# Split-precision expert products: one kind after the other instead of in turn, one cast by a transfer, one store moved

## The chip, the cores and the metric

One NeuronCore of a Trainium2 chip. The metric is the device time of one execution in microseconds (us), as the median of several runs.

## The reference, cut to what matters

```
x = attention(q, k, v, M_prev, z_prev, beta)     # 2304 tokens x 512
logits = x @ w_gate                              # 8 experts, 288 tokens each, greedily by logit
for e in range(8):
    h = maximum(x[mask_e] @ w1[e], 0)            # 512 -> 1024
    out[mask_e] = h @ w2[e]                      # 1024 -> 512
h = maximum(maximum(out @ m1, out @ m2), out @ m3)   # 512 -> 768, the same weights for all tokens
return h @ w_out                                 # 768 -> 512
```

## The kernel before, in words

The program has two stages. The first (attention, 0 to about 240 us of the span) the change leaves as it is. The second runs the routing and the experts one after the other, p = 0 to 7, each with its T = 288 tokens. A planner (`Plan.run`) orders the whole second stage: each task has a key, an engine, a guessed cost and dependences; at each step it takes the task that can start first, and of equals the one with the lowest key. The table `FK` holds the keys' offsets by kind of task, `R1KEY` that of the second routing round, `YSEQ` is new. What the planner gives is a fixed order of instructions on each engine; the engines then wait for each other only by semaphores.

Every matrix product is made to fp32 accuracy from three products: high by high in fp32r (weights in `whi` or `mh`, data in `xhi`, `hh`, `yh` or `gf`/`gc`), and two in bf16 (high by low and low by high, from `wlo`/`ml` and `xlo`/`hl`/`yl`). `mm3` issues the three in turn (lines 1429, 1431, 1432); the text calls them f, b, b, and a set of three a triple. A triple here streams 288 columns. Per expert there are

- h1: 8 blocks fb of 4 triples (d = 0 to 3), `fh1`, from the tokens into PSUM tile `w`; then ReLU and split into `hh`/`hl` (ACT line 1313, DVE 1319, ACT or DVE 1268),
- y: 8 blocks of 4 triples, `fy`, into four PSUM tiles `acc`; then the split into `yh`/`yl`,
- p: 18 blocks of 4 triples, `fp`, for f = 0 to 5 and three matrices i, into `w`; a maximum over i into `mt` (ACT 1550, DVE 1552) and a split,
- o: 18 triples of 512 columns, `fo`, into `acc`; then a copy and an indirect store by GpSimd's queue (line 1624).

That is 1,088 triples of 288 columns and 108 of 512 over the eight experts. In the order before, f, b and b of a triple stand together, two triples to a task; only the last y block and the first p block have tasks of two f and of four b.

The weights of an expert come in eight transfers of 512 KB (line 1361, queue of SP, tile `wraw`, three buffers). Each is split by halves: ACT casts to `whi` (1370), DVE takes the difference (1376), ACT casts the high part to bf16 (1380). The fourth transfer of expert 0 waits for the tokens' gather (1345). SP also stores each expert's row numbers to memory (`fi`, line 1512, tile `tidx` to `idxd`, 4 bytes at a time) and loads them back in another layout (`fj`, 1516). The weights shared by all tokens, `MH[k]` and `ML[k]` for k = 4 to 11, are split in the same stretch: ACT 1283, DVE 1289, ACT 1294.

Of the kernel before, what the change touches and what calls it, by code (L numbers as in the profile page):

```python
# [17 lines left out]
try:  # L18
# [27 lines left out]
RKEY = (-1000, -23.5)  # L46
FL0 = 3
NFILL = 88
R1, R1KEY = 9, 21.8
NK = 4  # L50
RSLACK = 300
CRIT, PATIENCE = -900, 0
GLAT, WLAT = 8500, 6000
FBUFS = {"wraw": 3, "whi": 4, "wlo": 4, "xo": 1, "xhi": 1, "xlo": 1, "w": 3, "acc": 4, "hh": 3, "hl": 3, "yh": 1, "yl": 1,
         "mt": 2, "ob": 3, "gc": 7, "gf": 2, "gcu": 7, "gfu": 2}
FK = {"m2": -600, "ml": 28.3, "load": -63.7, "w2": 17.1, "wsplit": -3.5, "gather": -148.1, "xt": -126.2, "h1": 0, "y": -46.8, "o": 13.0, "store": 103.5, "idx": -41.5}
# [1191 lines left out]
def experts(g, tc, plan, top, wr, xd, idxd, out):  # L1248
# [32 lines left out]
    for k in range(NK, 12):  # L1281
        def fh(e, k=k):
            A.copy(MH[k], g.W32[k])

        def flow(e, k=k, h=0):
            if h == 0:
                g.slot(k)
            q = slice(512 * h, 512 * h + 512)
            V.tensor_sub(ML[k][:, 0, q], g.W32[k][:, q], MH[k][:, q].bitcast(F32))

        t = add(FK["m2"] + k, {"ACT": act(1024)}, fh)
        for h in range(2):
            low = add(FK["ml"] + .1 * k + .05 * h, {"DVE": dve(512)}, lambda e, f=flow, h=h: f(e, h=h), [t, low, g.rounds[0].tt])
        low = add(FK["ml"] + .1 * k + .07, {"ACT": act(1024)}, lambda e, k=k: A.copy(ML[k][:, 1], MH[k].bitcast(F32)), [low])
        TM[k // 3].append(low)
    bfl, fo_ = Buf(R["acc"]), K()

# [33 lines left out]
    for p in range(E):  # L1331
# [92 lines left out]
            x.tx += list(split(kx + .1 * d, T, lambda o=o: o.pt[:, :T], hi, lambda i, x=x, d=d: x.xl[:, i, d], [td] + x.tx[:1],  # L1424
                               new=x.bx if d == 0 else [], use=[ob[d]] + ([] if d == 0 else x.bx)))

        def mm3(o, w, r, start, stop, part=(0, 1)):
            if 0 in part:
                nc.tensor.matmul(o, w[0], r[0], start=start, stop=False)  # L1429
            if 1 in part:  # L1430
                nc.tensor.matmul(o, w[2], r[1], start=False, stop=False)  # L1431
                nc.tensor.matmul(o, w[1], r[2], start=False, stop=stop)  # L1432

        def tri(h, l, d):
            return h[:, d], l[:, 0, d], l[:, 1, d]
# [6 lines left out]
        x.ty = []  # L1442
        hs = {}
        x.acc = [None] * 4
        ylast, yt = [], []
        for fb in range(8):
            bp, bhh, bhl = Buf(R["w"]), Buf(R["hh"]), Buf(R["hl"])
            o = K()
            kh = k0 + 2 * fb
            t = None  # L1450
            for hf in range(2):
                def fh1(e, x=x, fb=fb, hf=hf, o=o):
                    if hf == 0:
                        o.pt = ps.tile([128, 512], F32, name="w", bufs=FBUFS["w"])
                    for d in (2 * hf, 2 * hf + 1):
                        s = slice(d * 128, d * 128 + 128)
                        mm3(o.pt[:, :T], wts(x.W[fb], s), tri(x.xh, x.xl, d), d == 0, d == 3)

                t = add(kh + FK["h1"] + .1 * hf, {"PE": 760}, fh1, x.tw[fb, 0] + (x.tx[:6] if hf == 0 else x.tx + [t]), new=[bp] if hf == 0 else [],
                        use=([] if hf == 0 else [bp]) + x.bx + list(x.bw[fb]))  # L1460
# [19 lines left out]
            for hf, (fb, ts, o, bhh, bhl) in itertools.product(range(2), yt):  # L1480
                def fy(e, x=x, fb=fb, hf=hf, o=o, part=(0, 1)):
                    for d in (2 * hf, 2 * hf + 1):
                        if fb == 0:
                            x.acc[d] = ps.tile([128, 512], F32, name="acc", bufs=4)
                        s = slice(512 + d * 128, 512 + d * 128 + 128)
                        mm3(x.acc[d][:, :T], wts(x.W[fb], s), (o.a, (o.b[:, 0] if 1 in part else None), (o.b[:, 1] if 1 in part else None)), fb == 0, fb == 7, part)

                ky = k0 + 2 * fb + FK["y"] + .1 * hf if fb < 6 else k0 + 14 + FK["y"] + hf + .1 * (fb - 6)
                for part in ((0,), (1,)) if fb == 7 else ((0, 1),):
                    ylast.append(add(ky + .05 * part[0], {"PE": 270 * (0 in part) + 490 * (1 in part)}, lambda e, f=fy, part=part: f(e, part=part),  # L1490
                                     list(ts if 1 in part else ts[:1]) + x.tw[fb, 1] + ylast[-1:] + ([o[-1] for o in prev.ol] if prev else []),
                                     new=ya[2 * hf:2 * hf + 2] if fb == 0 else [],
                                     use=[bhh, bhl] + list(x.bw[fb]) + (ya[2 * hf:2 * hf + 2] if fb else [])))
# [12 lines left out]
        chunks = range(p * T // 128, (p + 1) * T // 128)
        oa = [Buf(R["acc"]) for _ in chunks]
# [7 lines left out]
            a, z = chunks[0], chunks[-1] + 1  # L1515
            nc.sync.dma_start(idx[:, a:z], idxd[a * 128:z * 128].rearrange("(c q) -> q c", q=128))

        t = add(k0 + FK["idx"], {"SP": 500}, fi, [r.tt] + x.tl[FL0:FL0 + 1], lat=2300)
        x.tidx = add(k0 + FK["idx"] + .1, {"SP": 500}, fj, [t], lat=2300)
        x.tm = []  # L1520
        for f in range(6):
            kf = k0 + 20 + 4 * f
# [2 lines left out]
            for i in range(3):  # L1525
                bp = Buf(R["w"])
                o = K()
                t = None
                for hf in range(2):
                    def fp(e, x=x, f=f, i=i, hf=hf, o=o, part=(0, 1)):  # L1530
                        if hf == 0 and 0 in part:
                            o.pt = ps.tile([128, 512], F32, name="w", bufs=FBUFS["w"])
                        for d in (2 * hf, 2 * hf + 1):
                            s = slice(d * F2 + f * 128, d * F2 + f * 128 + 128)
                            mm3(o.pt[:, :T], msub(i, s.start, 128), tri(x.yh, x.yl, d), d == 0, d == 3, part)

                    for part in ((0,), (1,)) if f == 0 and i == 0 else ((0, 1),):
                        need = x.ty[:6] if hf == 0 else x.ty + [t]
                        if part == (0,):
                            need = x.ty[6 * hf:6 * hf + 6:3] + ([t] if hf else [])  # L1540
                        elif part == (1,):
                            need = need + [t]
                        t = tp = add(kf + i + .1 * hf + .05 * part[0], {"PE": 270 * (0 in part) + 490 * (1 in part)},
                                     lambda e, f=fp, part=part: f(e, part=part), need + TM[i], new=[bp] if hf == 0 and 0 in part else [],
                                     use=([] if hf == 0 and 0 in part else [bp]) + x.by)
# [168 lines left out]
```

## Time and profile before

| | |
|---|---|
| median of 3 runs | 817.12 us (816.01 to 817.22) |
| profiled execution: time / span | 816.3 us / 814.6 us |
| PE busy | 783.8 us, 96% of the span |
| DVE, ACT busy | 578.6 us, 480.7 us |
| routing and start of expert 0 | 244 to 303 us of the span |
| experts, PE without a pause | 303 to 808 us |

The rows below are of the profiled execution, in us from the start of its span unless marked ns. A row of a timeline gives start, duration, engine, line, operation, output<-inputs, and in brackets the idle time of the engine just before it with what ended it. Matmuls overlap: a product's end (start plus duration) against the end of the one before it is what it adds.

### The profile page before, as it was taken

The page shows a single profiled execution, that of the slowest core. Times are in us where ns is not written, and L with a number is a line of the kernel's source. Part 1 is how long each engine was busy: PE and PEld are TensorE (multiplying, and loading weights), DVE is VectorE, ACT ScalarE, POOL GpSimd, SP SyncE. Part 2 cuts the span into 40 slices and gives each one's busy share as a digit, 9 for nine tenths or more (in the row PEclk, how much of TensorE's full clock was granted, in tenths as well). Part 3 has the DMA queues.
Part 4 walks back from the last instruction along what each step waited for, and adds up shares of the span by engine and source line. Part 5 has one row for each costly group of instructions (what it writes and reads, how often), then busy time and mean ns, then how long its engine had stood idle before and what let it go on. Part 6 is the DMA issues. An engine that isn't in the chain of part 4 may idle for free.

```text
span 814.6 us, 18746 instructions
## 1 busy us (share of the span) xinstructions
PE 783.8 (96%) x7022; PEld 623.4 (77%) x7022; DVE 578.6 (71%) x1780; ACT 480.7 (59%) x1238; POOL 107.6 (13%) x239
## 2 busy tenths in 40 slices
PE   8999999999986799999999999999999999999996
PEld 6899899899985567677777777767767777776773
DVE  7799999999557888688668757747856865643421
ACT  4678777777647673674564655546556465835521
POOL 2212222223101100201010210110101012001001
PEclk9999999999995899999999999999999999999999
DMA  7364746565013422322312320411331253421000
GB/s 239 91 220 153 238 130 233 177 219 169 23 60 93 110 51 79 107 79 96 116 53 79 107 79 30 157 54 39 104 107 54 78 134 107 132 25 52 2 1 39
DMA packets 39248, 83.79 MB, mean 103 GB/s; under 512 B 11454, under 2 KB 14198, under 8 KB 39158
## 3 DMA queue, kind: packets, MB, share of 16 engines
q1 hardware_dynamic: 35574, 72.87, 28.8%
q0 software_dynamic: 3584, 9.73, 4.0%
q8 instruction: 55, 0.90, 0.5%
q14 instruction: 35, 0.29, 0.1%
HBM read 72.77 MB, written 9.74 MB: 101 GB/s over the span
## 4 chain that ended last, share of the span: by engine, by line
PE 73%; issue 9%; DVE 8%; DMA 5%; ACT 3%; POOL 1%; SPq 1%; DVEq 0%; POOLq 0%; ACTq 0%
PE w L1431 12%; PE w L1429 12%; PE w L1432 11%; PE av L684 9%; PE acc L1429 6%; PE acc L1431 6%; PE acc L1432 5%; PE st L643 5%; PE rps L590 2%; PE rps L1148 2%; PE rps L543 1%; DMA wraw<-in_wr 1%; DVE junk L456 1%; DMA m2raw<-in_m2w 1%; PE w L1405 1%
## 5 line engine op out<-in xcount | busy, mean ns | idle before, releaser
L1429 PE MATMUL w<-yh,mh 128*128 128x288 f32 x576 | 219.8, 390 | 0.2 <-DVE mt L1552 0.2
L1431 PE MATMUL w<-yl,ml 128*128 128x288 bf16 x576 | 169.4, 296 | 0.0
L1432 PE MATMUL w<-yl,ml 128*128 128x288 bf16 x576 | 163.7, 286 | 0.0
L1429 PEld LDWEIGHTS w<-yh,mh 128*128 128x128 f32 x576 | 107.6, 190 | 17.9 <-DVE mt L1552 0.6
L684 PE MATMUL av<-V,pt 128*128 128x112 f32 (+1 forms) x960 | 105.0, 261 | 1.7 <-DVE nm L456 0.7
L684 PEld LDWEIGHTS av<-V,pt 128*128 128x128 f32 (+1 forms) x960 | 96.9, 173 | 6.4 <-issue 1.6
L1429 PE MATMUL w<-xhi,whi 128*128 128x288 f32 x256 | 100.3, 392 | 0.5 <-DVE xlo L1321 0.5
L1429 PE MATMUL acc<-hh,whi 128*128 128x288 f32 x256 | 95.9, 385 | 0.1
L1376 DVE TENSOR_TENSOR wlo<-wraw,whi 128x512 bf16<-128x512 f32 x128 | 84.2, 686 | 15.2 <-ACT whi L1370 14.4
L1552 DVE TENSOR_TENSOR mt<-w,mt 128x288 f32<-128x288 f32 x96 | 43.7, 455 | 66.3 <-PE w L1432 62.2
L1431 PEld LDWEIGHTS <-ml 128*128 128x128 bf16 x576 | 55.0, 96 | 39.0 <-issue 7.2
L1370 ACT CAST whi<-wraw 128x512 fp32r<-128x512 f32 x128 | 74.5, 617 | 17.4 <-PE acc L1429 9.1
L1431 PE MATMUL w<-xlo,wlo 128*128 128x288 bf16 x256 | 76.8, 300 | 1.9 <-ACT wlo L1380 1.9
L1380 ACT CAST wlo<-whi 128x512 bf16<-128x512 f32 x128 | 76.2, 616 | 0.0
L1431 PEld LDWEIGHTS <-wlo 128*128 128x128 bf16 x512 | 49.4, 96 | 34.4 <-ACT wlo L1380 2.4
L1431 PE MATMUL acc<-hl,wlo 128*128 128x288 bf16 x256 | 75.7, 298 | 0.0
L1432 PE MATMUL w<-xlo,wlo 128*128 128x288 bf16 x256 | 74.0, 289 | 0.0
L456 DVE CUSTOM_DVE_ANT_0 junk<-st,mask 128x512 bf16<-128x512 f32 (+3 forms) x128 | 62.6, 489 | 15.6 <-ACT pt L668 3.8
L1432 PE MATMUL acc<-hl,wlo 128*128 128x288 bf16 x256 | 73.1, 288 | 0.1
L1345 POOL DMA_INDIRECT xg<-xd,tidx x24 | 30.1, 1253 | 255.7 <-PE w L1432 233.3
L670 ACT ACTIVATE pt<-st 128x512 f32<-128x512 f32 x96 | 53.3, 601 | 14.2 <-PE st L643 13.2
L1432 PEld LDWEIGHTS <-ml 128*128 128x128 bf16 x576 | 57.1, 99 | 0.6
(283 smaller groups left out, 1699.2 us busy)
## 6 DMA issues: line engine op xcount, KB each, us to landing
wraw<-in_wr SPq DMA_DIRECT2D x64, 512.0 KB, 4.3
m2raw<-in_m2w SPq DMA_DIRECT2D x12, 512.0 KB, 5.2
V<-in_v SPq DMA_DIRECT2D x16, 365.0 KB, 5.3
KR<-in_kN SPq DMA_DIRECT2D x16, 288.0 KB, 3.1
QN<-in_qN SPq DMA_DIRECT2D x16, 288.0 KB, 3.1
vt<-in_vT SPq DMA_DIRECT2D x16, 288.0 KB, 5.1
xd<-x SPq DMA_DIRECT2D x16, 256.0 KB, 2.5
m2raw<-in_m2w SPq DMA_DIRECT2D x12, 256.0 KB, 3.1
```

Of the source, the lines that this page charges most:

```text
L456: V.tensor_tensor_reduce(out=junk[:, :w], in0=o.s[x][:, c:c + w], in1=m, scale=1.0, scalar=-3.0e38, op0=OP.add, op1=OP.max, accum_out=r.nm ...
L643: PE.matmul(d[:kr, c:c + z - a], neg[q, :kr] if wt is None else wt[q, k], mv[q, a:z], start=x == 0, stop=x == 3)
L670: A.activation(r.PT[:, i, 512 * gi:512 * gi + 512], o.t[i], AF.Exp, scale=0.125)
L684: PE.matmul(AV[:m, i, j * C:j * C + w], r.PT[:, i, o:o + m], r.V[:, c:c + w], start=kb == 0, stop=kb == j)
L1345: g.gather = G.indirect_dma_start(out=x.xg[:96, c], out_offset=None, in_=xd, in_offset=bass.IndirectOffsetOnAxis(ap=r.tidx[:96, c:c + 1], ...
L1370: A.copy(x.W[fb][0][:, q], x.RAW[fb][:, q])
L1376: V.tensor_sub(x.W[fb][1][:, 0, q], x.RAW[fb][:, q], x.W[fb][0][:, q].bitcast(F32))
L1380: A.copy(x.W[fb][1][:, 1, q], x.W[fb][0][:, q].bitcast(F32))
L1429: nc.tensor.matmul(o, w[0], r[0], start=start, stop=False)
L1431: nc.tensor.matmul(o, w[2], r[1], start=False, stop=False)
L1432: nc.tensor.matmul(o, w[1], r[2], start=False, stop=stop)
L1552: V.tensor_max(q.mt, o.pt[:, :T], q.mt)
```

## The change

Line numbers of the changed kernel are higher by up to 18 (1429 becomes 1441, 1431 and 1432 become 1443 and 1444, 1361 becomes 1371, 1512 and 1516 become 1535 and 1539).

```diff
-R1, R1KEY = 9, 21.8
+R1, R1KEY = 9, 19.9
+YSEQ = ((0, 0, (0, 1, 2, 3)), (0, 1, (0, 1)), (1, 0, (0, 1)), (1, 1, (0, 1)), (0, 1, (2, 3)), (1, 0, (2, 3)), (1, 1, (2, 3)))
-FK = {"m2": -600, "ml": 28.3, "load": -63.7, "w2": 17.1, ...
+FK = {"m2": -600, "ml": 28.9, "load": -59.3, "w2": -38.7, ...
...
+        if k == NK:
+            def fhb(e, k=k):
+                g.slot(k)
+                G.dma_start(ML[k][:, 1], MH[k].bitcast(F32))
+
+            hb = add(-699, {"POOL": 1100}, fhb, [t], lat=8000)
...
+        if k > NK:
+            low = add(FK["ml"] + .1 * k + .07, {"ACT": act(1024)}, lambda e, k=k: A.copy(ML[k][:, 1], MH[k].bitcast(F32)), [low])
+        else:
+            TM[k // 3].append(hb)
...
-        def mm3(o, w, r, start, stop, part=(0, 1)):
-            if 0 in part:
+        ALL, HALF = ((0, (0, 1, 2, 3)), (1, (0, 1, 2, 3))), ((0, (0, 1)), (1, (0, 1)), (0, (2, 3)), (1, (2, 3)))
+
+        def mms(part, o, w, r, start, stop):
+            if part == 0:
                 nc.tensor.matmul(o, w[0], r[0], start=start, stop=False)
-            if 1 in part:
+            else:
                 nc.tensor.matmul(o, w[2], r[1], start=False, stop=False)
                 nc.tensor.matmul(o, w[1], r[2], start=False, stop=stop)
...
-            for hf in range(2):
+            for n, (part, ds) in enumerate(HALF if fb == 0 and p == 0 else ALL):
...
-                    for d in (2 * hf, 2 * hf + 1):
+                    for d in ds:
                         s = slice(d * 128, d * 128 + 128)
-                        mm3(o.pt[:, :T], wts(x.W[fb], s), tri(x.xh, x.xl, d), d == 0, d == 3)
+                        mms(part, o.pt[:, :T], wts(x.W[fb], s), tri(x.xh, x.xl, d), d == 0, d == 3)
...
+            seq = [(i, part, ds) for i in range(len(yt)) for part, ds in (HALF if fb == 0 else ALL)]
+            if fb == 7:
+                seq = YSEQ
...
-        t = add(k0 + FK["idx"], {"SP": 500}, fi, [r.tt] + x.tl[FL0:FL0 + 1], lat=2300)
-        x.tidx = add(k0 + FK["idx"] + .1, {"SP": 500}, fj, [t], lat=2300)
+        t = add(k0 + FK["idx"], {"SP": 500}, fi, [r.tt] + (x.tl[FL0:FL0 + 1] if p else x.tl[7:]), lat=11000)
+        x.tidx = add(k0 + FK["idx"] + .1, {"SP": 500}, fj, [t], lat=5000)
...
-                for hf in range(2):
+                for n, (part, ds) in enumerate(HALF if f == 0 else ALL):
...
-                    mm3(x.oc[ci], [a[:, w:w + 128] for a in (h.t, h.u[:, 0], h.u[:, 1])], msub(3, s.start, DM), f == 0, f == 5)
+                    for part in range(2):
+                        mms(part, x.oc[ci], [a[:, w:w + 128] for a in (h.t, h.u[:, 0], h.u[:, 1])], msub(3, s.start, DM), f == 0, f == 5)
```

A block of h1, y or p is now one task of its four f (`part` 0) and one of its eight b (`part` 1); `HALF` blocks are cut in two by d. The triples of o keep their order. `ML[4]`'s high part is cast by a transfer from SBUF to SBUF on GpSimd's queue, no longer by ACT. The numbers in `FK` shift other tasks; `w2` lets the second half of a weight block be split directly behind the first.

The order on PE, at a p block of the second expert (tile `w`; `mh6` to `mh8` and `mh0` to `mh2` are pieces of the shared weights). Before:

```order
L1429 MATMUL w_5136<-yh_4903,mh6_4130 128x288
L1431 LDWEIGHTS ml_4594
L1431 MATMUL w_5136<-yl_4904,ml_4594 128x288
L1432 LDWEIGHTS ml_4594
L1432 MATMUL w_5136<-yl_4904,ml_4594 128x288
L1429 MATMUL w_5136<-yh_4903,mh7_4131 128x288
```

and after the change, the same kind of place:

```order
L1441 MATMUL w_5235<-yh_4901,mh6_4130 128x288
L1441 MATMUL w_5235<-yh_4901,mh7_4131 128x288 x2
L1441 MATMUL w_5235<-yh_4901,mh8_4132 128x288
L1441 MATMUL w_5243<-yh_4901,mh0_973 128x288
L1441 MATMUL w_5243<-yh_4901,mh1_1162 128x288
L1441 MATMUL w_5243<-yh_4901,mh2_1437 128x288 x2
L1443 LDWEIGHTS ml_4620
L1443 MATMUL w_5235<-yl_4902,ml_4620 128x288
L1444 LDWEIGHTS ml_4620
L1444 MATMUL w_5235<-yl_4902,ml_4620 128x288
```

The planner has put the f tasks of two blocks together: eight f into two tiles `w`, and behind them sixteen b. Over the second stage, an f of 288 columns stood directly behind another 46 times before and 887 times now; directly behind a routing product of 8 columns or fewer, or a transpose, 74 times and 46 times, a b 10 and 34 times.

The order on SP, from the sixth weight transfer of expert 0 (ISA rows set the address; `ei` is the number of the second expert). Before:

```order
L1361 DMA wraw<-in_wr 128x1024
L1512 DMA idxd<-tidx 96x3x1
L1361 ISA
L1361 DMA wraw<-in_wr 128x1024
L1516 DMA idx<-idxd 128x2x1
L1361 ISA
L1361 DMA wraw<-in_wr 128x1024
L1337 TENSOR_LOAD ei
```

and now:

```order
L1371 DMA wraw<-in_wr 128x1024
L1371 ISA
L1371 DMA wraw<-in_wr 128x1024
L1371 ISA
L1371 DMA wraw<-in_wr 128x1024
L1535 DMA idxd<-tidx 96x3x1
L1539 DMA idx<-idxd 128x2x1
L1347 TENSOR_LOAD ei
```

The store and the load of the row numbers have moved behind the seventh and the eighth weight transfer. On POOL the casting transfer stands between the attention's last stores and the first gather:

```order
L873 DMA xd<-xl 128x4x128
L873 DMA xd<-xl 64x128
L1296 DMA ml<-mh_4128 128x1024
L1355 DMA xg<-xd,tidx 96x512 x6
L1641 MEMSET spacer 1x1
```

Nothing else on POOL has moved.

## Rows read from the trace of the kernel before

**Rows 1.** Busy time by stretch: us, then busy (xcount) by engine, PEclk, DMA, GB/s
```profile
244.00:272.00 28.00, 16.35 (x208) 14.24 (x208) 20.65 (x86) 15.32 (x37) 7.25 (x5) 0.65 0.35 88
272.00:303.00 31.00, 28.52 (x231) 21.43 (x231) 26.38 (x49) 25.95 (x53) 0.00 (x0) 0.88 0.42 86
303.00:744.00 441.00, 440.66 (x3623) 328.30 (x3624) 303.52 (x911) 246.59 (x614) 41.73 (x51) 1.00 0.27 84
744.00:808.00 64.00, 63.41 (x446) 45.18 (x444) 21.71 (x54) 26.55 (x63) 2.03 (x5) 1.00 0.05 17
```

**Rows 2.** Who PE waited for from 303 to 808: total us, times, longest
```profile
PE w L1429 <- DVE mt L1552: 0.2, 1, 0.2
```

**Rows 3.** Timeline of PE, triples in turn, first and last of 19
```profile
754.57 0.39 PE L1429 MATMUL w<-xhi,whi 128*128 128x288 f32 x1
754.80 0.30 PE L1431 MATMUL w<-xlo,wlo 128*128 128x288 bf16 x1
754.93 0.29 PE L1432 MATMUL w<-xlo,wlo 128*128 128x288 bf16 x1
...
762.02 0.39 PE L1429 MATMUL acc<-hh,whi 128*128 128x288 f32 x1
```

**Rows 4.** Timeline of PE where bf16 stands behind bf16, fp32r behind fp32r
```profile
505.00 0.29 PE L1431 MATMUL w<-yl,ml 128*128 128x288 bf16 x1
...
505.37 0.29 PE L1432 MATMUL w<-yl,ml 128*128 128x288 bf16 x1
505.40 0.39 PE L1429 MATMUL w<-yh,mh 128*128 128x288 f32 x1
...
506.18 0.64 PE L1429 MATMUL w<-yh,mh 128*128 128x288 f32 x3
```

**Rows 5.** Timeline of PE behind a routing product of 8 columns
```profile
283.46 0.17 PE L1158 MATMUL rps<-fl,ones 128*128 128x8 bf16 x1
283.48 0.38 PE L1429 MATMUL acc<-hh,whi 128*128 128x288 f32 x1
...
503.44 0.17 PE L1164 MATMUL rps<-fl,ones 128*128 128x8 bf16 x1
503.47 0.28 PE L1431 MATMUL acc<-hl,wlo 128*128 128x288 bf16 x1
```

**Rows 6.** Weight loads: one group of the page, and the timeline of PEld
```profile
L1429 PEld LDWEIGHTS w<-yh,mh 128*128 128x128 f32 x576 | 107.6, 190 | 17.9 <-DVE mt L1552 0.6
...
506.16 0.44 PEld L1429 LDWEIGHTS w<-yh,mh 128*128 128x128 f32 x3
```

**Rows 7.** Timeline of SP's queue: expert 0, then the second expert's first loads
```profile
279.66 0.43 SPq L1512 DMA_DIRECT2D idxd<-tidx  x1
282.56 0.35 SPq L1361 DMA_DIRECT2D wraw<-in_wr  x1
288.93 0.40 SPq L1516 DMA_DIRECT2D idx<-idxd  x1
289.58 0.34 SPq L1361 DMA_DIRECT2D wraw<-in_wr  x1
...
315.92 0.92 SPq L1361 DMA_DIRECT2D wraw<-in_wr  x2
```

**Rows 8.** Who waited: timelines of ACT and PE, then the landing times of `wraw`
```profile
292.74 1.14 ACT L1370 CAST whi<-wraw 128x512 fp32r<-128x512 f32 x2 [2.28 <-DMA wraw<-in_wr]
...
286.54 0.30 PE L1431 MATMUL w<-xlo,wlo 128*128 128x288 bf16 x1 [0.34 <-ACT wlo L1380]
...
295.40 0.30 PE L1431 MATMUL w<-xlo,wlo 128*128 128x288 bf16 x1 [1.59 <-ACT wlo L1380]
...
DMA to landing us min/median/max: 3.3/4.3/10.0
```

**Rows 9.** Busy time by stretch around the pause (columns as in the first group)
```profile
276.00:296.50 20.50, 18.55 (x169) 14.27 (x168) 17.06 (x33) 18.20 (x36) 0.00 (x0) 1.00 0.54 102
296.50:300.00 3.50, 3.50 (x17) 2.39 (x16) 3.49 (x8) 3.50 (x8) 0.00 (x0) 0.51 0.00 0
```

**Rows 10.** Timelines of POOL and ACT before the first gather, and a transfer's landing
```profile
244.85 2.53 POOL L872 DMA_DIRECT2D xd<-xl  x2 [10.32 <-ACT xl L795]
263.62 2.35 POOL L1345 DMA_INDIRECT xg<-xd,tidx  x1 [16.24 <-DVE R L1245]
...
246.17 7.70 ACT L1283 CAST mh<-w 128x1024 fp32r<-128x1024 f32 x8
...
xd<-xl POOLq DMA_DIRECT2D x1, 256.0 KB, 5.0
```

**Rows 11.** Timelines of ACT and DVE at the split between y and p
```profile
502.17 0.40 ACT L1268 CAST yh<-acc 128x288 fp32r<-128x288 f32 x1 [0.97 <-PE acc L1432]
...
502.60 0.46 DVE L1321 TENSOR_TENSOR yl<-acc,yh 128x288 bf16<-128x288 f32 x1 [0.89 <-ACT yh L1268]
```

More of the change, by code (lines that the diff above doesn't have):

```diff
@@ L55 @@
          "mt": 2, "ob": 3, "gc": 7, "gf": 2, "gcu": 7, "gfu": 2}
-FK = {"m2": -600, "ml": 28.3, "load": -63.7, "w2": 17.1, "wsplit": -3.5, "gather": -148.1, "xt": -126.2, "h1": 0, "y": -46.8, "o": 13.0, "store": 103.5, "idx": -41.5}
+FK = {"m2": -600, "ml": 28.9, "load": -59.3, "w2": -38.7, "wsplit": -3.5, "gather": -148.1, "xt": -118.5, "h1": 0, "y": -46.8, "o": 12.9, "store": 103.5, "idx": -51.1}
 BUFS = {"KR": 2, "QN": 3, "MZ": 2, "V": 3, "VT": 2, "phi": 1, "ph": 1, "KH": 3, "QH": 3, "KL": 3, "QL": 3, "QJ": 2, "NM": 2, "nm": 2, "nmr": 2,
@@ L1285, in flow @@
         def flow(e, k=k, h=0):
-            if h == 0:
+            if k not in ML:
                 g.slot(k)
@@ L1291, in experts @@
         t = add(FK["m2"] + k, {"ACT": act(1024)}, fh)
-        for h in range(2):
-            low = add(FK["ml"] + .1 * k + .05 * h, {"DVE": dve(512)}, lambda e, f=flow, h=h: f(e, h=h), [t, low, g.rounds[0].tt])
-        low = add(FK["ml"] + .1 * k + .07, {"ACT": act(1024)}, lambda e, k=k: A.copy(ML[k][:, 1], MH[k].bitcast(F32)), [low])
+        if k == NK:
[3 more added lines that the diff above has]
+            hb = add(-699, {"POOL": 1100}, fhb, [t], lat=8000)
+        for h in range(2):
+            low = add(FK["ml"] + .1 * k + .05 * h, {"DVE": dve(512)}, lambda e, f=flow, h=h: f(e, h=h), [t, low, g.rounds[0].tt] + ([hb] if k == NK else []))
+        if k > NK:
+            low = add(FK["ml"] + .1 * k + .07, {"ACT": act(1024)}, lambda e, k=k: A.copy(ML[k][:, 1], MH[k].bitcast(F32)), [low])
+        else:
+            TM[k // 3].append(hb)
         TM[k // 3].append(low)
@@ L1425, in experts, with cost @@
                                new=x.bx if d == 0 else [], use=[ob[d]] + ([] if d == 0 else x.bx)))
-        def mm3(o, w, r, start, stop, part=(0, 1)):
-            if 0 in part:
+        ALL, HALF = ((0, (0, 1, 2, 3)), (1, (0, 1, 2, 3))), ((0, (0, 1)), (1, (0, 1)), (0, (2, 3)), (1, (2, 3)))
+        def mms(part, o, w, r, start, stop):
+            if part == 0:
                 nc.tensor.matmul(o, w[0], r[0], start=start, stop=False)
-            if 1 in part:
+            else:
                 nc.tensor.matmul(o, w[2], r[1], start=False, stop=False)
                 nc.tensor.matmul(o, w[1], r[2], start=False, stop=stop)
+        def cost(part, ds):
+            return len(ds) * (245 if part else 133) + (0 if part else 14)
         def tri(h, l, d):
@@ L1444, in experts @@
         x.acc = [None] * 4
-        ylast, yt = [], []
+        ylast, yt, x.yd = [], [], {}
         for fb in range(8):
@@ L1450, in experts, with fh1 @@
             t = None
-            for hf in range(2):
-                def fh1(e, x=x, fb=fb, hf=hf, o=o):
-                    if hf == 0:
+            for n, (part, ds) in enumerate(HALF if fb == 0 and p == 0 else ALL):
+                def fh1(e, x=x, fb=fb, o=o, part=part, ds=ds):
+                    if not hasattr(o, "pt"):
                         o.pt = ps.tile([128, 512], F32, name="w", bufs=FBUFS["w"])
-                    for d in (2 * hf, 2 * hf + 1):
+                    for d in ds:
                         s = slice(d * 128, d * 128 + 128)
-                        mm3(o.pt[:, :T], wts(x.W[fb], s), tri(x.xh, x.xl, d), d == 0, d == 3)
-                t = add(kh + FK["h1"] + .1 * hf, {"PE": 760}, fh1, x.tw[fb, 0] + (x.tx[:6] if hf == 0 else x.tx + [t]), new=[bp] if hf == 0 else [],
-                        use=([] if hf == 0 else [bp]) + x.bx + list(x.bw[fb]))
+                        mms(part, o.pt[:, :T], wts(x.W[fb], s), tri(x.xh, x.xl, d), d == 0, d == 3)
+                need = x.tw[fb, 0][:1] + [x.tx[3 * d] for d in ds]
+                if part:
+                    need = x.tw[fb, 0] + [y for d in ds for y in x.tx[3 * d:3 * d + 3]]
+                t = add(kh + FK["h1"] + .05 * n, {"PE": cost(part, ds)}, fh1, need + [t], new=[] if n else [bp],
+                        use=([bp] if n else []) + x.bx + list(x.bw[fb]))
             def ha(o=o):
@@ L1479, in experts, with fy @@
                 continue
[L1480 to L1483, printed above, removed]
+            seq = [(i, part, ds) for i in range(len(yt)) for part, ds in (HALF if fb == 0 else ALL)]
+            if fb == 7:
+                seq = YSEQ
+            for n, (i, part, ds) in enumerate(seq):
+                yb, ts, o, bhh, bhl = yt[i]
+                def fy(e, x=x, fb=yb, o=o, part=part, ds=ds):
+                    for d in ds:
+                        if fb == 0 and part == 0:
                             x.acc[d] = ps.tile([128, 512], F32, name="acc", bufs=4)
                         s = slice(512 + d * 128, 512 + d * 128 + 128)
[L1486 to L1493, printed above, removed]
+                        mms(part, x.acc[d][:, :T], wts(x.W[fb], s), (o.a, o.b[:, 0] if part else None, o.b[:, 1] if part else None), fb == 0, fb == 7)
+                ky = k0 + 2 * yb + FK["y"] + .05 * n if fb < 7 else k0 + 14 + FK["y"] + .1 * n
+                ylast.append(add(ky, {"PE": cost(part, ds)}, fy, (list(ts) + x.tw[yb, 1] if part else [ts[0], x.tw[yb, 1][0]]) + ylast[-1:] +
+                                 ([o[-1] for o in prev.ol] if prev else []), new=[ya[d] for d in ds] if yb == 0 and part == 0 else [],
+                                 use=[bhh, bhl] + list(x.bw[yb]) + ([ya[d] for d in ds] if yb or part else [])))
+                for d in ds:
+                    x.yd[d] = ylast[-1]
             yt = []
@@ L1503, in experts @@
             x.ty += list(split(k0 + 18 + .1 * d, T, lambda x=x, d=d: x.acc[d][:, :T], hi, lambda i, x=x, d=d: x.yl[:, i, d],
-                               [ylast[-4 + d // 2 * 3]] + x.ty[:1], new=x.by if d == 0 else [], use=[ya[d]] + ([] if d == 0 else x.by)))
+                               [x.yd[d]] + x.ty[:1], new=x.by if d == 0 else [], use=[ya[d]] + ([] if d == 0 else x.by)))
         chunks = range(p * T // 128, (p + 1) * T // 128)
@@ L1528, in experts, with fp @@
                 t = None
-                for hf in range(2):
-                    def fp(e, x=x, f=f, i=i, hf=hf, o=o, part=(0, 1)):
-                        if hf == 0 and 0 in part:
+                for n, (part, ds) in enumerate(HALF if f == 0 else ALL):
+                    def fp(e, x=x, f=f, i=i, o=o, part=part, ds=ds):
+                        if not hasattr(o, "pt"):
                             o.pt = ps.tile([128, 512], F32, name="w", bufs=FBUFS["w"])
-                        for d in (2 * hf, 2 * hf + 1):
+                        for d in ds:
                             s = slice(d * F2 + f * 128, d * F2 + f * 128 + 128)
[L1535 to L1545, printed above, removed]
+                            mms(part, o.pt[:, :T], msub(i, s.start, 128), tri(x.yh, x.yl, d), d == 0, d == 3)
+                    need = [y for d in ds for y in x.ty[3 * d:3 * d + 3]] if part else [x.ty[3 * d] for d in ds]
+                    t = tp = add(kf + i + .05 * n, {"PE": cost(part, ds)}, fp, need + [t] + TM[i], new=[] if n else [bp],
+                                 use=([bp] if n else []) + x.by)
                 def fm(e, i=i, o=o, q=q):
```

## The prediction

> **What bounds the kernel now.** I read the busy time by stretch first, because the share over the whole span mixes two stages [rows 1]. From 303 to 744 us PE is busy 440.66 of 441 us, and from 744 to 808 it is busy 63.41 of 64. The view of waits over that stretch names a single one of 0.2 us [rows 2]. So for 505 us whatever PE needs less comes off the end, unless another engine becomes late: DVE is busy 303.52 us and ACT 246.59 us of the 441. The granted clock there is 1.00, the upper level of 2.4 GHz. Ahead of 303 it is different: from 272 to 303, expert 0, PE is busy 28.52 of 31 us at a mean clock of 0.88. There a change counts by what it does to the waits.
>
> Next I read what one product costs in that full stretch. Durations overlap, so I go by distances and ends. Nineteen triples in turn take 762.02 - 754.57 = 7.45 us, 0.392 us each [rows 3]. Inside a run of bf16 products the starts are (505.37 - 505.00)/3 = 0.123 us apart [rows 4]. One f lasts 0.39 us and a run of three 0.64 us, so each f behind an f adds 0.125 to 0.13 us [rows 4]. If the kinds changed only once, a triple would cost 0.13 + 2 x 0.123 = 0.376 us. The other 0.016 us is paid for changing: in rows 4 the b before ends at 505.66 and the f at 505.79, 0.13 later, and in rows 3 the first b ends at 755.10, 0.14 behind the f's 754.96, where one in a run adds 0.12.
>
> **The change part by part.**
>
> *Order by kind.* No product is added or removed. The built orders have 46 f of 288 columns behind an f before, and 887 now: 841 triples give up their changes. 841 x 0.016 = 13.5 us. The rows are written to 0.01 us; with the f run at 0.125 the saving is 0.021 a triple, and with the triple at 0.390 and the run at 0.133 it is 0.011. So the bounds are 9 and 18 us.
>
> *Behind routing products.* An f directly behind an 8-column product ends 283.86 - 283.63 = 0.23 us after it, 0.10 more than behind an f; a b ends 503.75 - 503.61 = 0.14 after it, 0.02 more than in a run [rows 5]. There are 28 such f fewer (74 to 46) and 24 such b more (10 to 34): 28 x 0.10 - 24 x 0.02 = 2.3 us saved. The o triples keep their order, and the few changes of kind beside them are within 0.5 us either way; taken as nothing.
>
> PE therefore needs 15.8 us less. 128 of the 1,088 triples, h1 and y of expert 0, lie ahead of 303 us, but the sum below takes only pauses from there, so nothing is counted twice.
>
> *The row numbers behind the eighth weight load.* The store of 4-byte pieces is issued at 279.66 and its reload can start only at 288.93, so it is under way for some 9 us [rows 7]. The seventh weight transfer, issued at 282.56 behind it, lands when ACT's wait of 2.28 us ends, at 292.74: 10.2 us, where the median is 4.3 [rows 7, 8]. PE pauses 1.59 us for it, and 0.34 us earlier [rows 8]. Behind that pause the granted clock falls to 0.51, the lower level of 1.2 GHz, from 296.5 to 300 [rows 9]; half of 3.5 us is 1.7 us of lost work. With the store moved, the seventh transfer should land at about 282.6 + 4.3 = 286.9, before it is wanted, and the pause and the fall of the clock go: 1.59 + 0.34 + 1.7 = 3.6 us. What is late next is ACT itself, busy 18.20 of 20.50 us there [rows 9]; I leave it 0.6 us and take 3.0. Bounds: 0, if ACT takes the transfer's place, and 3.6. The reload and the second expert's number now wait on SP until the store lands, some 9 us after the eighth load, near 297 us; queued behind them are only the second expert's loads, which before were first issued at 315.92, once its number was known [rows 7]. That is hidden.
>
> *The casting transfer.* It takes one cast of 128 x 1024 (about 1 us, 7.70/8 [rows 10]) off ACT, at a place where ACT then waits for weights anyway: no gain. On POOL it starts when the first `mh` cast is done, near 247 us, and the first gather comes at 263.62 [rows 10]. No row shows such a transfer; the nearest is `xd<-xl`, 256 KB in 5.0 us [rows 10]. Twice that is 10 us and ends before 258. From below it costs nothing, from above, at half that rate, 20 us, it would still be moving at 267 and hold up the gathers by some 3 us. I take 0.
>
> *Keys.* The second half of a weight block is split directly behind the first, which frees `wraw` buffers earlier; R1KEY and the rest shift work between DVE and ACT, which have slack after 303. Taken as nothing.
>
> *New waits.* A block's result now comes only with the last of its eight b, and f run ahead into a second tile. The tight place is between y and p: the last y product of the first two d is 10 products (1.25 us) ahead of the first p product. The split needs about 0.2 + 0.40 for the first `yh`, 0.43 more until the difference is on its way and 0.46 for it [rows 11], and the four f that go first (0.53 us) cover the rest. I allow 0.2 us an expert, 1.5 us in all; bounds 0 and 6.
>
> Sum: -13.5 - 2.3 - 3.0 + 1.5 = **-17.3 us**. The profiled execution took 816.3, so 799.0; the median stands 0.8 above it, so about **800 us**. With the bounds of the larger terms the forecast's own range is 794 to 806.
>
> **A rule against it.** By rows 3 and 4 a triple costs 0.392 us in turn and 0.376 us in runs. The Trainium skill, "TensorE: Matmul & The Clock Gate", section "Back-to-back issue gap", gives a warm matmul N/2.4 + 2.5 ns, by its columns alone: 0.1225 us for each of the three, whatever stands before it. By that, order is worth nothing. The trace agrees for b behind b (0.123) and disagrees for a triple in turn (0.392 and not 0.368).
>
> **The rivals.**
>
> *A. The saving is partly taken back by waits* (0.13). Results come later and in bunches; with PE 3% faster, ACT or DVE is late at p's maxima and at y's split. Against it: DVE and ACT are busy 69% and 56% of the full stretch [rows 1]. For it: before, PE waited only 0.2 us there, so the order fitted, and this one is new. At 1 us an expert more, 800 + 8 = 808.
>
> *B. Order is worth nothing* (0.06): the 0.016 us belong to every f and go with it into the runs. Then only the start gains: 817.1 - 3.0 + 1.0 = 815. Against it stand the runs of three in rows 4, but they are short.
>
> *C. Long runs of f are bound by their weight loads, and it gets slower* (0.03). An fp32r weight load lasts 190 ns, against a stream of 0.12 us [rows 6]. A run of two or three might live on loads made ahead; in a run of eight each f would cost 0.19. 841 x (0.19 - 0.13) = 50 us: 850. It decides from 0.13 + 17.3/841 = 0.151 us an f. Against it: three loads in a row take 0.44 us, 0.125 for each after the first [rows 6]. By the same page's section "LDWEIGHTS", a load of 128 columns takes 128/1.2 = 107 ns, under the stream; the rows lie nearer to that than to 190.
>
> *D. Expert 0 gets worse* (0.06): the moved splits make ACT or DVE late in 272 to 303, another pause, and the clock falls again. The start then costs 3 us instead of giving 3: 806.
>
> **How the numbers follow.** The forecast has 0.72, and A to D the rest. The range for 8 in 10 is 793 to 812: the forecast, D and most of A; B and C are left out. About 0.2%, 1.6 us, can be told from no change. Slower takes C and the far end of A, waits of 2.4 us or more an expert (0.04): 0.07. The same is the edge of A and B: 0.04. Faster: 0.89.
>
> **What would show it.** Right: ends in runs of eight f 0.13 us apart and of sixteen b 0.122; PE still busy nearly all of the time from expert 0's p on, for about 490 us instead of 505; the seventh and eighth weight transfers landing in about 4 us; no wait of ACT for `wraw` near 290 us and a granted clock of 1.00 from 276 us on. Wrong: f ends 0.14 us or more apart in runs (B, C), waits for `yl`, `mt` or `hh` of over 6 us in all (A), a low clock after 280 us (D), or a gather that is issued later than 264 us. The forecast is wrong as a whole if PE's busy time from expert 0's p to the end falls by less than 8 us.

## The result and the profile after

| | before | after |
|---|---|---|
| median | 817.17 us (816.01 to 818.25, 4 runs) | 798.51 us (797.01 to 798.56, 4 runs) |
| ratio, 95% interval | | 0.9768 [0.975, 0.9785] |
| span of the profiled execution | 814.6 us | 796.8 us |

The forecast was 800.0 us. The busy time of the changed kernel by stretch (columns as in [rows 1]):

```profile
272.00:303.00 31.00, 30.17 (x261) 25.11 (x262) 29.38 (x60) 27.63 (x56) 0.00 (x0) 0.92 0.27 86
303.00:744.00 441.00, 439.50 (x3706) 354.04 (x3728) 303.68 (x911) 257.18 (x648) 48.22 (x52) 1.00 0.31 86
744.00:790.00 46.00, 45.14 (x313) 33.78 (x315) 12.69 (x36) 13.88 (x38) 1.51 (x3) 1.00 0.01 3
```

PE is about as full as before, and the end has moved forward by 18 us. The view of waits names nothing that PE waited for from 303 to 789 us. From 272 to 303 it names three:

```profile
PE w L1441 <- DVE xlo L1331: 0.5, 1, 0.5
PE w L1415 <- DMA xg<-xd,tidx: 0.5, 1, 0.5
PE w L1443 <- ACT wlo L1390: 0.3, 1, 0.3
```

The two pauses of 0.34 and 1.59 us for `wlo` [rows 8] have shrunk to one of 0.3. The timeline of PE in a p block shows the new unit, eight f and sixteen b:

```profile
385.13 0.29 PE L1444 MATMUL w<-yl,ml 128*128 128x288 bf16 x1
385.16 1.31 PE L1441 MATMUL w<-yh,mh 128*128 128x288 f32 x8
386.31 0.30 PE L1443 MATMUL w<-yl,ml 128*128 128x288 bf16 x1
...
388.16 0.29 PE L1444 MATMUL w<-yl,ml 128*128 128x288 bf16 x1
388.19 0.49 PE L1441 MATMUL acc<-mh,gc 128*128 128x512 f32 x1
```

Read the ends. The eight f take from 385.42 to 386.47, 0.131 us each; the first b adds 0.14; the other fifteen go from 386.61 to 388.45, 0.123 each. Eight triples take 388.45 - 385.42 = 3.03 us, 0.379 each, against 0.392 in turn [rows 3]. The timelines of SP and of ACT at the seventh weight block:

```profile
258.45 30.57 SPq L1371 DMA_DIRECT2D wraw<-in_wr  x8
289.06 0.47 SPq L1535 DMA_DIRECT2D idxd<-tidx  x1
297.88 0.41 SPq L1539 DMA_DIRECT2D idx<-idxd  x1
313.02 1.53 SPq L1371 DMA_DIRECT2D wraw<-in_wr  x3
```
```profile
291.08 0.61 ACT L1380 CAST whi<-wraw 128x512 fp32r<-128x512 f32 x1
```

All eight weight loads now go out ahead of the store, and ACT's cast has no wait in front of it. By the semaphore updates in the trace, the last part of the seventh load lands at 287.17, 3.5 us behind its issue at 283.64; before it was 292.72 - 282.56 = 10.2 us. (The 10.0 in the landing line of [rows 8] is another load, of the last expert, issued at 710.54; the changed kernel still has two such, of 10.0 and 10.2 us, for later experts.) The store still takes 297.88 - 289.06 = 8.8 us until its reload can start, and no load of expert 0 stands behind it. The granted clock around expert 0 (to set beside [rows 9]):

```profile
272.00:277.00 5.00, 4.50 (x20) 3.82 (x20) 4.21 (x9) 4.64 (x12) 0.00 (x0) 0.53 0.37 108
277.00:302.00 25.00, 24.67 (x235) 20.37 (x234) 24.16 (x49) 21.98 (x44) 0.00 (x0) 1.00 0.26 86
```

The lower level of 1.2 GHz is left shortly before 277, as before, and does not come back at 296.5.

**Where the 17.8 us of span went.** I cut both traces at the same events. From the first product of p of expert 0 to the end of the last product of o: 501.83 us before, 487.38 after, 14.45 less. From the first h1 product to the first p product: 33.08 and 28.76, 4.32 less. The rest goes the other way by 1.0: the first gather is issued 0.52 later, its issue to the first h1 product takes 0.26 more (9.13 for 8.87), and behind the last product it takes 0.21 more (7.39 for 7.18).

### The profile page after: what moved, and what is told of

Same layout as the page of the kernel before. It is cut to its first block, busy times and chain, and to the rows that moved or that the text cites. A ratio compares the mean times of both kernels' runs of the same rounds, so it can differ in the third digit from the quotient of the medians.

```text
span 796.8 us, 18726 instructions
## 1 busy us (share of the span) xinstructions
PE 767.2 (96%) x6996; PEld 642.8 (81%) x7022; DVE 572.5 (72%) x1771; ACT 479.4 (60%) x1246; POOL 114.8 (14%) x240
## 4 chain that ended last, share of the span: by engine, by line
PE 73%; issue 10%; DVE 9%; ACT 3%; DMA 2%; POOL 1%; SPq 0%; DVEq 0%; POOLq 0%; ACTq 0%
PE w L1441 12%; PE w L1443 11%; PE w L1444 11%; PE av L685 9%; PE acc L1441 6%; PE acc L1444 6%; PE acc L1443 5%; PE st L644 5%; PE rps L591 2%; DVE junk L457 2%; PE rps L1149 2%; PE rps L544 1%; DMA QN<-in_qN 1%; PE w L1415 1%; PE st L444 1%
## 5 line engine op out<-in xcount | busy, mean ns | idle before, releaser
L1443 PE MATMUL w<-yl,ml 128*128 128x288 bf16 x576 | 146.3, 287 | 0.1
L1444 PE MATMUL w<-yl,ml 128*128 128x288 bf16 x576 | 145.6, 286 | 0.0
L1441 PE MATMUL w<-yh,mh 128*128 128x288 f32 x576 | 103.5, 313 | 0.0
L1441 PEld LDWEIGHTS w<-yh,mh 128*128 128x128 f32 x576 | 81.8, 189 | 4.2 <-ACT mt L1567 0.4
L1355 POOL DMA_INDIRECT xg<-xd,tidx x24 | 36.7, 1531 | 248.4 <-PE w L1444 223.3
L1443 PE MATMUL acc<-hl,wlo 128*128 128x288 bf16 x256 | 66.9, 288 | 0.0
L1444 PE MATMUL acc<-hl,wlo 128*128 128x288 bf16 x256 | 66.2, 286 | 0.0
L1443 PE MATMUL w<-xlo,wlo 128*128 128x288 bf16 x256 | 65.8, 288 | 0.3 <-ACT wlo L1390 0.3
L1444 PE MATMUL w<-xlo,wlo 128*128 128x288 bf16 x256 | 65.6, 287 | 0.0
L1443 PEld LDWEIGHTS <-wlo 128*128 128x128 bf16 x512 | 49.9, 98 | 16.7 <-ACT wlo L1390 0.5
L1444 PEld LDWEIGHTS <-wlo 128*128 128x128 bf16 x512 | 50.3, 98 | 10.1
L1323 ACT ACTIVATE hh<-w 128x288 fp32r<-128x288 f32 x64 | 26.3, 411 | 52.5 <-PE w L1444 52.3
```

The source lines that it names most:

```text
L1355: g.gather = G.indirect_dma_start(out=x.xg[:96, c], out_offset=None, in_=xd, in_offset=bass.IndirectOffsetOnAxis(ap=r.tidx[:96, c:c + 1], ...
```

## The experiments

**The three parts alone and in pairs.** The change has three parts, and with before and after every combination was run; the planner's keys are a fourth part, which was not run by itself. `order_only` is the changed kernel without the other two; `store_only` and `cast_only` are the kernel before with one part. These three keep the keys (`FK`, `R1KEY`) of before. `all_but_order` is the kernel before with store, cast and the new keys.

```diff
# store_only: the kernel before, and
-        t = add(k0 + FK["idx"], {"SP": 500}, fi, [r.tt] + x.tl[FL0:FL0 + 1], lat=2300)
+        t = add(k0 + FK["idx"], {"SP": 500}, fi, [r.tt] + (x.tl[FL0:FL0 + 1] if p else x.tl[7:]), lat=11000)
# cast_only: the kernel before, and for k == NK
+                G.dma_start(ML[k][:, 1], MH[k].bitcast(F32))
...
```

> The order by kind alone, with the store, the cast and the keys as before. Theory (changes of kind cost PE some 16 ns each): PE's part from expert 0's p on falls by about 14 us as in the changed kernel; the pause for the seventh weight transfer of expert 0 stays or grows by 1 to 2 us, since the planner now sets store and reload ahead of it, so -12 to -15 us, 802 to 805. Rival (the gain needs the new keys, which keep waits away): many small waits of PE in p, -5 us or less, 812 or more.

> Only the store and reload of the row numbers moved behind the eighth weight transfer. Theory: the seventh transfer lands in about 4 us, PE's pause of 1.6 us and the half clock behind it go, -2.5 to -3.6 us, 813.5 to 814.7. Rival (ACT or DVE takes the transfer's place): another pause in expert 0, 0 to -1 us, 816 to 817.

> Only the casting transfer on GpSimd's queue in place of one cast on ACT. Theory: hidden, and what it takes off ACT lay in idle time: within 0.7 us of before, 816.5 to 817.8. Rival (it delays the gathers behind it on POOL's queue, the first matmul of expert 0 begins 0.5 us or more later, as it began 0.77 us later in the changed kernel): +0.5 to +3 us, 817.7 to 820.

> Store, cast and keys of the change, products in turn as before. Theory: only the start gains, -2.5 to -4 us, 813 to 814.7, and the triples still take 0.39 us each. Rival (keys and cast carry a good part of the gain): -6 us or more, 811 or less.

Two more take one part out of the changed kernel again: `store_back` (the two lines of `fi` and `fj` as before) and `no_cast` (ACT casts `ML[4]`). Both have the new keys. `after_again` is their neighbour on the same chip.

> The changed kernel itself, on the same chip as the three runs beside it, so that each of them has it as its neighbour: 798.5 us, within 0.8, or 0.977 of the kernel before.

> The changed kernel with the store and the reload of the row numbers put back ahead of expert 0's last weight loads; the instructions of the four computing engines are the same, in the same order. If the store's own transfer holds up the weight load behind it, the pause of expert 0 comes back and the start stretch (first f product to the first product of p) grows from 28.8 us to 30 to 32.5: 800.0 to 802.0 us in all. Rival: the pause is set by ACT's and DVE's work and the weight load is late for another reason: within 0.4 us of the changed kernel.

> The changed kernel with the second copy of m2's fifth piece made by ACT again, not by a transfer on GpSimd's queue. If the casting transfer is worth nothing, as predicted: 798.5 within 0.5 us. If the gather, which is 0.2 us longer and 0.5 us later in the traces with the transfer, sets the start: 797.8 to 798.2, with the first f product at 272.6 and not 273.3. If ACT's missing 1 us copy was what kept expert 0 free of waits: 799.2 to 800.5, with ACT waits at 285 to 300.

Here "start" is from the first h1 product to the first p product, and "full" from there to the last o product, in us of the profiled execution.

| order | store | cast | kernel | median | ratio to before, 95% | start | full |
|---|---|---|---|---|---|---|---|
| | | | before | 817.17 | 1 | 33.08 | 501.83 |
| | x | | store_only | 813.80 | 0.9946 [0.9929, 0.9963] | 29.62 | 502.74 |
| | | x | cast_only | 817.68 | 0.999 [0.998, 0.9999] | 31.32 | 503.78 |
| | x | x | all_but_order | 815.59 | 0.9964 [0.995, 0.9978] | 29.92 | 503.26 |
| x | | | order_only | 802.43 | 0.9806 [0.9789, 0.9822] | 31.16 | 489.22 |
| x | x | | no_cast | 798.50 | 0.9752 [0.9739, 0.9765] | 27.92 | 488.82 |
| x | | x | store_back | 800.44 | 0.9782 [0.9769, 0.9795] | 28.98 | 488.34 |
| x | x | x | after_again | 799.78 | 0.9767 [0.9753, 0.978] | 29.26 | 488.31 |

(The medians of before beside them were 818.91 us for `store_only`, `cast_only`, `all_but_order` and `order_only` and 818.68 for the last three, so rows are compared by their ratios.) "Start" and "full" are of one trace each, and differ from trace to trace: `after` and `after_again` are the same kernel, 0.9 us apart in the full stretch; `no_cast_again`, below, is `no_cast`, and its start is 28.86 for 27.92, with the lower clock lasting 5.9 us into expert 0 and not 3.6.

The medians of `order_only`, `store_only`, `cast_only` and `store_back` fell into their expected ranges. Those of `all_but_order` (815.59 for 813 to 814.7) and `after_again` (799.78 for 797.7 to 799.3) lay above theirs. `no_cast` came out at the 798.5 of the cast that is worth nothing, but 1.28 us below its neighbour, which that did not foresee. In `order_only` the pause for the seventh load was expected to stay or grow; ACT waits 0.13 us there, and the view of PE's waits names none for `wlo`. Three things follow.

*The order is the change.* The four kernels without it take 501.8 to 503.8 us in the full stretch, the four with it 488.3 to 489.2, and after itself 487.4. Store and cast take nothing off there.

*Store and cast overlap.* Where nothing else differs: in the kernel before, the store alone is worth 0.54% (4.4 us) and the cast alone 0.1% (0.8 us). In the changed kernel, `store_back` gives back only 0.7 us, with overlapping ranges (799.75 to 802.32 and 799.08 to 800.26). What covers the store, the cast or the order, the runs don't settle. From `order_only` to `no_cast`, both with the new order and without the cast, the ratio falls by 0.54% again, which points to the cast; but these two differ in their keys as well, and part of the start of `order_only` is its lower clock, which lasts 6.1 us into expert 0. My expectation for `store_back`, 800.0 to 802.0 with a pause, held in its number and failed in its mechanism. Its timelines of SP and of ACT:

```profile
277.80 0.42 SPq L1535 DMA_DIRECT2D idxd<-tidx  x1
283.93 0.35 SPq L1371 DMA_DIRECT2D wraw<-in_wr  x1
287.64 0.39 SPq L1539 DMA_DIRECT2D idx<-idxd  x1
```
```profile
291.06 0.40 ACT L1323 ACTIVATE hh<-w 128x288 fp32r<-128x288 f32 x1
291.37 0.61 ACT L1380 CAST whi<-wraw 128x512 fp32r<-128x512 f32 x1
```

The store is ahead of the seventh load again, and the load is late again: by the semaphore updates it lands at 291.09, 7.2 us behind its issue. In the three other traces in which the load is issued while the store ahead of it is under way it takes 10.2 (before), 8.1 (`cast_only`) and 9.8 us (`mirror`, below); in `after`, `after_again`, `store_only`, `all_but_order` and `no_cast`, with the store behind it, 3.3 to 3.5. But ACT comes to that block at 291.37 straight from other work, with no wait, as it does in the changed kernel at 291.08. The late transfer is covered, by 0.28 us.

*The casting transfer costs 0.45 us in two places; whether the whole is a loss beside the moved store stays open.* `no_cast` was 1.28 us faster than its neighbour. That was measured once side by side, and the two intervals of the ratios overlap. What repeats is smaller. In the six traces with the transfer the first gather's issue to the first h1 product takes 9.09 to 9.16 us and the tail behind the last product 7.38 to 7.40; in the six traces without it, all with the same number of fillers (idle matmuls that keep PE busy until the gathered rows land), 8.86 to 8.95 and 7.16 to 7.18. That is 0.45 us in all. The gathers on POOL, first `no_cast`, then the changed kernel:

```profile
263.41 2.35 POOL L1346 DMA_INDIRECT xg<-xd,tidx  x1 [16.28 <-DVE R L1246]
266.06 1.02 POOL L1346 DMA_INDIRECT xg<-xd,tidx  x1 [0.30 <-issue]
267.39 1.36 POOL L1346 DMA_INDIRECT xg<-xd,tidx  x1 [0.30 <-issue]
```
```profile
247.80 0.62 POOL L1296 DMA_DIRECT2D ml<-mh  x1 [0.17 <-issue]
264.14 2.31 POOL L1355 DMA_INDIRECT xg<-xd,tidx  x1 [15.72 <-DVE R L1246]
266.76 1.53 POOL L1355 DMA_INDIRECT xg<-xd,tidx  x1 [0.30 <-issue]
268.59 1.08 POOL L1355 DMA_INDIRECT xg<-xd,tidx  x1 [0.30 <-issue]
```

With the transfer ahead, the second gather takes 1.53 us on POOL in place of 1.02, so the third starts 4.45 us behind the first and not 3.98. The transfer itself was issued 16 us earlier; why the second gather is longer these rows don't show.

**Half the changes of kind, in the old schedule.** `order_only` changes the planner's tasks and its order along with the kinds. `mirror` is the kernel before with every second triple the other way round, so that f stand in pairs; no task, key or other engine differs.

```diff
+            if flip:
+                nc.tensor.matmul(o, w[2], r[1], start=start, stop=False)
+                nc.tensor.matmul(o, w[1], r[2], start=False, stop=False)
+                nc.tensor.matmul(o, w[0], r[0], start=False, stop=stop)
+                return
...
-                        mm3(o.pt[:, :T], wts(x.W[fb], s), tri(x.xh, x.xl, d), d == 0, d == 3)
+                        mm3(o.pt[:, :T], wts(x.W[fb], s), tri(x.xh, x.xl, d), d == 0, d == 3, flip=d % 2)
```

> The kernel before with the three products of every second triple of h1, y and p in the mirrored order (bf16, bf16, fp32r), so that fp32r products stand in pairs; no task, key, wait or other engine is touched. f products behind a b product fall from 919 to 544, b behind f from 1,037 to 534. If the change of kind is what the order costs, PE's time falls by 7.1 us (by the ns of each pair of kinds in the trace of before), about half of what the whole order by kind gave: a ratio of 0.990 to 0.993. If the gain of the order by kind came from the planner's new order of blocks, or from its finer waits: 0.998 to 1.002.

Measured: 809.75 us (808.93 to 812.71), ratio 0.9925 [0.9901, 0.9949]. It is inside the expected range and its interval ends below the rival's 0.998, so the kinds' order gives time with the schedule untouched. In the full stretch it takes 497.09 us, 4.74 less than before: somewhat over a third of the 12.61 of `order_only`, not half. That the ratio still met its range is luck: another 1.69 us come from the start (31.39 for 33.08), in which the clock did not fall. Its timeline of PE, two pairs of triples:

```profile
745.37 0.30 PE L1436 MATMUL acc<-hl,wlo 128*128 128x288 bf16 x1
...
745.75 0.29 PE L1430 MATMUL acc<-hl,wlo 128*128 128x288 bf16 x1
745.77 0.39 PE L1431 MATMUL acc<-hh,whi 128*128 128x288 f32 x1
746.00 0.29 PE L1434 MATMUL w<-xhi,whi 128*128 128x288 f32 x1
746.14 0.30 PE L1436 MATMUL w<-xlo,wlo 128*128 128x288 bf16 x1
```

From first b to first b, 746.14 - 745.37 = 0.77 us for two triples, 0.385 each. The ends of the last four rows are 746.04, 746.16, 746.29 and 746.44: the f add 0.12 and 0.13, and the b behind them 0.15. Over all rows the medians are 0.132 us for an f of 288 columns behind an f, 0.129 (before) or 0.132 (`mirror`) for one behind a b, 0.138 to 0.139 for a b behind an f and 0.122 for a b behind a b. So the price of a change sits in the b behind the f. Pairs of 288-column products take 5.6 us less in the full stretch where 7.1 were expected, half of what they save in the changed kernel (11.4, below); products of the routing behind them take 1.2 us more, and so only 4.74 comes off.

That makes a series, each value read at the places where such runs happen to stand. Over the second stage, the median time of a triple, from the end of one run of b to the end of the next, is 0.390 us in turn (890 cases before), 0.385 in mirrored pairs (365), and in the changed kernel 0.383, 0.381, 0.3795 and 0.379 for runs of two, four, six and eight f (10, 18, 21 and 32 cases). Each doubling of the run saves less: from four to eight it is 0.002 us. (The mean in turn is 0.392 us from expert 0's p on, as in [rows 3], and 0.379 to 0.381 in runs of four and more.)

Expert 0 of `mirror` shows a pause like that of before, and no fall of the clock behind it (the timeline of PE, and the busy time by stretch as in [rows 9]):

```profile
294.03 0.30 PE L1436 MATMUL w<-xlo,wlo 128*128 128x288 bf16 x1 [1.51 <-ACT wlo L1380]
```
```profile
296.50:300.00 3.50, 3.33 (x38) 2.68 (x37) 3.50 (x6) 2.77 (x6) 0.00 (x0) 1.00 0.00 0
```

**The rest of the order.** `osplit` gives the triples of o two tasks each, so that the planner can put their f beside other f.

```diff
-                    for part in range(2):
-                        mms(part, x.oc[ci], [a[:, w:w + 128] for a in (h.t, h.u[:, 0], h.u[:, 1])], msub(3, s.start, DM), f == 0, f == 5)
+                for part in range(2):
...
+                    x.ol[ci].append(add(kf + FK["o"] + .1 * ci + OK * part, {"PE": (226, 440)[part]}, fo, (h.ts if part else h.ts[::3]) + TM[3] + x.ol[ci][-1:],
```

> The changed kernel with the products of o in two tasks each, one per kind, so that the planner can put the 512-column f products beside other f products. By the ns of each pair of kinds in the trace of before the PE time falls by 1.8 us: 796.0 to 798.0 us. Rival: the smaller tasks let the planner choose an order that waits for the splits of mt, which gives it back: 798.5 to 800, with waits for gf and gc on PE.

Measured: 803.23 us (802.56 to 803.57), ratio 0.9807 [0.9794, 0.9821]: 3.45 us slower than `after_again` beside it. Both the forecast and the rival's place were wrong. Who PE waited for from 303 to 795 us:

```profile
PE acc L1442 <- ACT hh L1324: 2.3, 4, 0.8
PE acc L1444 <- DVE hl L1330: 2.1, 3, 0.7
```

```profile
428.15 0.29 PE L1445 MATMUL w<-xlo,wlo 128*128 128x288 bf16 x1
428.93 0.54 PE L1442 MATMUL acc<-hh,whi 128*128 128x288 f32 x2 [0.50 <-ACT hh L1324]
```

In the changed kernel PE waits for nothing there, and for `hh` 0.5 us in `after_again`. The waits stand at y products that need the split of h1, not at the splits of `mt`: three times (428.9, 563.5 and 628.7 us) at the last h1 block of an expert, once at 541.8, where `after_again` has its 0.5 too. At the three places the y products of the last block stand directly behind its h1 products (the two rows above); in `after_again` four f and four b of the y block before and 18 products of the routing stand between them. So the smaller tasks of o let the planner choose an order that took this cover away. It is a wait of rival A's kind, at a place A did not name. The 1.8 us did not show either: without its 4.4 us of waits the full stretch of `osplit` would be 492.25 - 4.4 = 487.9 us, and that of `after_again` without its 0.5 is 487.8.

**More cover for the gather.** The changed kernel runs its first 3.5 us of expert 0 at 1.2 GHz, as the one before did. `more_fill` is `no_cast` with more of the idle matmuls; `no_cast_again` is its neighbour.

```diff
-NFILL = 88
+NFILL = 110
```

> The changed kernel without the casting transfer, again, as the neighbour of the next run: a ratio of 0.975 to the kernel before.

> The changed kernel without the casting transfer and with 110 instead of 88 of the idle matmuls that keep PE busy until the gathered rows land: 8 of the 22 come ahead of the first transposes, 14 between the first and the second. If the half clock of 269.1 to 275.9 us follows from PE's idle time at 265 to 269, it goes or comes shorter, and the first products of expert 0 run at full clock: 1 to 2.5 us less than its neighbour. Rival: the clock falls all the same, or the fillers hold up the transposes: 0 to 0.5 us more.

Measured: `no_cast_again` 798.52 us (797.76 to 798.98), ratio 0.9774 [0.9751, 0.9797], and `more_fill` 798.99 (798.85 to 799.5), 0.9782 [0.976, 0.9805]. The rival held. The timeline and the busy time of `more_fill`:

```profile
267.25 0.47 PE L1406 MATMUL w<-ident,xg 96*128 96x96 f32 x3 [2.30 <-DMA xg<-xd,tidx]
267.55 0.25 PE L1406 MATMUL acc<-ident,xg 96*128 96x96 f32 x1
267.63 1.51 PE L1302 MATMUL acc<-ones 128*128 128x128 bf16 x14
```
```profile
267.50:270.00 2.50, 2.28 (x22) 1.99 (x20) 1.36 (x3) 0.00 (x0) 0.53 (x1) 0.57 0.44 134
```

PE still idles 2.30 us for the gather, and the clock still falls. The fillers behind the first transposes then run mostly at the low level, last 1.51 us, and from the gather to the first h1 product it takes 9.42 us instead of 8.95.

**What is best.** `no_cast`, the change without its casting transfer, has the lowest ratio once, 0.9752 (798.50 us); measured again on another chip it has 0.9774 (798.52 us), no better than the 0.9768 and 0.9767 of the change itself. So whether it beats the change, by the 1.3 us of the one side by side comparison, by the 0.45 us that repeat in the traces, or not at all, the runs leave open.

## Why the prediction was right

The forecast was 800.0, in a range of 793 to 812; the time was 798.5. Step by step:

- *What bounds the kernel.* Right. PE's need in the full stretch set the time, and all of what it gave up came off the end.
- *Order by kind, -13.5.* Right in mechanism, a little too large. I added up what each product's end adds to the one before it, from expert 0's p to the end: pairs of 288-column products 384.8 us before and 373.4 after, 11.4 less. That is 0.0136 for each of the 841 triples and not 0.016. The 0.392 of a triple in turn held as a mean; the 0.376 in runs was too cheap, for in runs of four and more a triple takes 0.379 to 0.381: an f behind an f adds 0.132, and each run still has one expensive b, which the 0.376 left out. The working also gave 128 triples ahead of 303 us; by its own loops h1 and y of one expert are 64. The sum did not use it.
- *Behind routing products, -2.3.* Right: f and b of 288 columns behind such a product or a transpose took 16.7 us before and 14.3 after, 2.4 less. Pairs with a 512-column product gave another 0.8, where I had taken nothing.
- *New waits, +1.5.* Not there: the view of waits from 303 to 789 us is empty in the changed kernel and names 0.5 us in `after_again`. That made up for the order's term: -13.5 - 2.3 + 1.5 = -14.3, measured -14.45. That the sum is so close is luck: the order's term was 2.1 us too large, and 1.5 us of waits did not come.
- *The store behind the eighth weight load, -3.0.* The sign and size are right for what the step described: alone it gave 4.4 us by its ratio, 3.46 in the start stretch. But beside the cast, in the changed kernel, it is worth 0.7 by medians: in `store_back` ACT comes to the seventh block 0.9 us later than before (291.37 for 292.74 - 2.28 = 290.46) and the load lands 1.6 us earlier (291.09 for 292.72). The term's lower bound, 0 if ACT takes the transfer's place, allowed for that. Together the three parts gave 4.3 us in the start stretch, 1.3 more than the term, and the later gather and the longer tail took 1.0 back, which the sum did not have. The step failed in pricing a part by itself and adding it to parts that shorten the same wait. The clock's fall, 1.7 us of the term, went, but `mirror` has the pause without the fall, so the pause alone does not bring it; of the kernel before there is one trace, so how often the fall comes is not known.
- *The casting transfer, 0.* A little off: alone it goes with 0.8 us less, barely clear of noise (0.998 to 0.9999), and with no pause for the seventh load (ACT waits 0.17 us for it), for a cause that the runs don't show; beside the moved store it costs 0.45 us in the gathers and the tail. The mark I had set, a gather issued after 264 us, was touched (264.14), but tells nothing: cast_only's stood at 263.91, all_but_order's at 263.57.

The rivals. A did not come with this order; a wait of its kind came with the next one (`osplit`). B falls: `mirror` gains with the schedule untouched. The Trainium skill, "TensorE: Matmul & The Clock Gate", section "Back-to-back issue gap", gives N/2.4 + 2.5 ns, which is 0.1225 us for each of these products, by its columns alone, and calls it the gap of an isolated product. For b behind b the traces agree (0.122), for b behind f (0.139) and for f (0.129 to 0.132) they don't. C falls: f in runs of eight end 0.131 apart, though each of their weight loads lasts 189 ns (a group of the profile's page, to set beside [rows 6]). D did not come.

```profile
L1441 PEld LDWEIGHTS w<-yh,mh 128*128 128x128 f32 x576 | 81.8, 189 | 4.2 <-ACT mt L1567 0.4
```

## What to carry to other kernels

Where PE is full, price a product by the product ahead of it, from ends in the trace: here a bf16 product behind an fp32r one cost 0.017 us more, and grouping by kind had most of its worth at runs of four. Price two parts that shorten the same wait together, and run each of them in the company it will have: the store's move was worth 4.4 us alone and 0.7 in the changed kernel. An order that leaves no wait may still have no slack: in `osplit`, cutting the tasks of o finer let the planner move away the products that had covered the split of h1.

## What was not expected

- The cost of alternating lies on one side. A b behind an f adds 0.139 us where one behind a b adds 0.122; an f adds 0.129 to 0.132 behind either.
- A transfer that casts on GpSimd's queue, issued 16 us ahead, goes with 0.22 us more until the first gathered rows are used and 0.22 us more behind the last product, in all six traces that have it.
- A pause of 1.5 to 1.6 us in expert 0 came with a fall of the granted clock to 0.51 in before and without one in `mirror`.
